# Raw x^T of the first token group by DMA transposes from DRAM, with eight h chunks on it and six on normalized x

## The chip, the cores and the metric

The kernel runs on one core of a Trainium2 chip. The metric is device time in microseconds; the number compared is the median over runs. One further execution was recorded by the profiler, and all views of the profile are of that one.

## The reference

The input x has 2048 tokens of 448 features in bf16. Both branches work on the same layer-normalized x, and the result of one gates the other:

```
xn  = layernorm(x)
q, k, v = split(xn @ wqkv)               # 16 heads of 28
pq, pk  = phi(q), phi(k)                 # phi(t) = (t > 0 ? t + 1 : exp(t)) + 1e-6
s   = (pq @ (pk^T v)) / (pq . sum(pk)) @ wo      # per head, not causal
h   = relu(xn @ w1 + b1)^2               # 1792 wide
g   = silu(h @ w2 + b2)
out = x + s * g
```

## The kernel before

**Tiling.** The 2048 tokens are 16 tiles of 128 (`x_tok[:, si]`), four groups of four. Features lie on partitions in four slices: three of 128 and a rest of 64, which is kept twice, on the lower and the upper 64 partitions, so that the rests of two units run as a pair of half-row matmuls. Normalized x (`xn`) is written by DVE (`ln_norm`, L489), its rest is doubled (L498), and DMA transposes issued by SP (L503, two tiles each) turn it into `xT`, which all matmuls of x read. K units (`kk`, L589) make one token tile of k, Q units (`qq`, L611) one 128-feature slice of q for a group, and h chunks (`hh`, L669) one of the fourteen 128-wide slices of h for a group. ACT applies a ReLU (L638, L641) and DVE or ACT squares (L646, L647). `gg(si)` (L1016) multiplies a token tile of h by w2, and DVE takes the sum out of PSUM (L1034 for group 0, L1041 for the others).

**The first group.** So that TensorE needn't wait for the layer norm, all fourteen h chunks of group 0 are computed from x that isn't normalized (raw x). After some warm-up matmuls (`warm`, L1143) TensorE transposes two x tiles at a time against an identity matrix (`raw_transpose`, L687 to L690); DVE and ACT copy the result out of PSUM into `xr` (L697, L702). Chunks 0 to 3 run in two halves of 256 tokens (L663), one after each transpose. The mean is taken out afterwards: `col_sums(p)` (L723 to L732) sums the columns of w1's part p and adds b1, `stat_rows` and `row_transpose` (L798, L805) make rows of means and deviations, and `aug` (L812) adds their product to the chunk. The factor 1/deviation is left out of h, and its square is applied by `gg` of group 0 through `rvar`:

```
out=gs, in0=ps(b)[:, 0:D], scalar=rvar[:, si : si + 1], in1=b2b[:, :], op0=ALU.mult, op1=ALU.add
```

**Order of work.** Every operation is added to a program in an order written by hand at the end of the kernel. TensorE and SP keep that order. ACT, DVE and POOL are ordered by a planner (`schedule`), which simulates with estimated durations and picks, among what is ready, the operation with the least due time (`late`, derived from the TensorE order), or the one whose `prio` is set. PSUM's eight banks are handed out in the same simulation. A queue waits in its order: an instruction that isn't ready holds up all behind it.

**Queues.** SP issues x tiles 0-1 and 2-3, b1row, w1 part 1, x tiles 4-7, w1 parts 2 and 3, the K and Q weights (wk, wq) and b1r, and after them the transposes as they come due. ACT issues w1 part 0 only. (Part p of w1 holds the columns of chunks 4p to 4p+3.) Token s of partition p is row p*16 + s of x.

Of the kernel before, what the change touches and what calls it, by code (L numbers as in the profile page):

```python
# [9 lines left out]
P = 128  # L10
# [18 lines left out]
class Op:  # L29
    def __init__(self, eng, emit, reads, writes, dur, alts, nbytes):  # L30
        self.eng, self.emit, self.dur, self.alts, self.nbytes = eng, emit, dur, alts, nbytes
        self.reads, self.writes = list(reads), list(writes)
        self.raw, self.deps, self.succ = set(), set(), []
        self.start = self.end = None
        self.seq = None
        self.late = 1e9
        self.prio = None
        self.sync = None
        self.fence = False


class Program:
# [5 lines left out]
    def __init__(self):  # L48
        self.ops, self.writer, self.readers = [], {}, {}
        self.aliases = {}  # L50

# [3 lines left out]
    def add(self, eng, emit, reads=(), writes=(), dur=0.2, alts=(), nbytes=0):  # L55
        reads = [p for r in reads for p in self.aliases.get(r, (r,))]
        op = Op(eng, emit, reads, writes, dur, alts, nbytes)
        for t in op.reads:
            w = self.writer.get(t)
            if w is not None:  # L60
                op.raw.add(w)
            self.readers.setdefault(t, []).append(op)
        for t in op.writes:
            w = self.writer.get(t)
            if w is not None and w is not op:
                op.deps.add(w)
            for r in self.readers.get(t, ()):
                if r is not op:
                    op.deps.add(r)
            self.writer[t] = op  # L70
            self.readers[t] = [r for r in self.readers.get(t, ()) if r is op]
        op.raw.discard(op)
        op.deps |= op.raw
        for d in op.deps:
            d.succ.append(op)
        self.ops.append(op)
        return op

    def schedule(self):
# [6 lines left out]
        for op in reversed(ops):  # L86
# [6 lines left out]
            op.late = late - op.dur - LAT if op.prio is None else op.prio  # L93
# [40 lines left out]
        while n:  # L134
# [69 lines left out]
            if op.nbytes:  # L204
# [72 lines left out]
def bass_recurrent_scan__linear_attn_block__dense_activation_squared_relu__prompt_kernel(  # L277
    nc, A_x, A_wqkv, A_wo, B_x, B_w1, B_b1, B_w2, B_b2, out
):
    with ExitStack() as es:  # L280
# [10 lines left out]
        ones = sb("ones", [P, 1], bf)  # L291
        onesr = sb("onesr", [1, P], bf)
# [8 lines left out]
        xr = sb("xr", [P, 4, 512], bf)  # L301
        xT = sb("xT", [P, NT, 4, P], bf)
# [62 lines left out]
        vset(onesr[:, :], 1.0, "onesr")  # L365
# [6 lines left out]
        vset(bsel[:, 3:5], 1.0, "bsel", True)  # L372
        add(
# [35 lines left out]
        x_r = A_x[0].rearrange("(p s) d -> p s d", s=NT)  # L409
        o_r = out[0].rearrange("(p s) d -> p s d", s=NT)  # L410

        def dma(eng, dst, src, writes, nbytes, reads=(), dur=0.45):
            add(eng, lambda e, _: e.dma_start(dst, src), reads, writes, dur, nbytes=nbytes)

        def load_x(lo, hi, eng="sp"):
            dma(eng, x_tok[:, lo:hi, :], x_r[:, lo:hi, :], [("x", i) for i in range(lo, hi)], (hi - lo) * P * D * 2)
# [29 lines left out]
        load_x(0, 2)  # L446
        load_w1(0, "act", "act")
        load_x(2, 4)
        dma("sp", b1row[:, :], B_b1.rearrange("(o f) -> o f", o=1), ["b1row"], F * 2)
        load_w1(1, "sp", "sp")  # L450
        load_x(4, 8)
        load_w1(2, "sp", "sp")
        load_w1(3, "sp", "sp")
        load_k("sp", w_qkv, A_wqkv, "wk", D, 2 * D)
        load_k("sp", w_qkv, A_wqkv, "wq", 0, D)
        dma("sp", b1r[:, :], B_b1.rearrange("(f p) -> f p", p=P), ["b1r"], F * 2)
# [39 lines left out]
        def x_transpose(lo, hi):  # L496
# [11 lines left out]
            )  # L508
# [41 lines left out]
        def pe_two(a, b, close=True):  # L550
# [10 lines left out]
            if close:  # L561
                a[3]()
                b[3]()

# [70 lines left out]
        def h_out(b, g, fi):  # L635
            slot = r2[:, fi, g * 512 : (g + 1) * 512]
            if g == 0:
# [12 lines left out]

        def hh(g, fi, full=True):
            b = Buf("H")

            def mm(e, rw, c, start, stop, part=None):
# [4 lines left out]
                if g == 0:  # L659
                    rhs = xr[rw, c, :]  # L660
                    if part is not None:
                        t = slice(256 * part, 256 * part + 256)
                        return e.matmul(  # L663
                            ps(b)[:, t], lhs, xr[rw, c, t], start=start and part == 0, stop=False,
                            skip_group_check=True,
                        )
                else:
                    rhs = xT[rw, 4 * g : 4 * g + 4, c, :]
                return e.matmul(ps(b)[:, 0:512], lhs, rhs, start=start, stop=stop)  # L669

            reads = (["xr"] if full else []) if g == 0 else xnames(g)
            return b, reads + w1names(fi // 4), mm, lambda: h_out(b, g, fi), 512

        def raw_transpose(lo):
            bs = [Buf("T"), Buf("T")]
            t = slice(lo * P, lo * P + 256)

            def f(e, _):
                last = None
                for i, b in enumerate(bs):  # L680
                    v = ps(b)[:, :].bitcast(bf)
                    for c in (2 * i, 2 * i + 1):
                        for k in (0, 1):
                            o = ((c - 2 * i) * 2 + k) * P
                            xs = x_tok[:, lo + k, :]
                            if c < 3:
                                last = e.transpose(v[:, o : o + P], xs[:, c * P : (c + 1) * P], ident[:, :])  # L687
                            else:
                                e.transpose(v[:, o : o + P], xs[:, 320:448], ident[:, :])
                                last = e.transpose(v[0:64, o : o + P], xs[:, 384:448], ident[:, :])  # L690
                return last

            add("pe", f, [("x", lo), ("x", lo + 1), "ident"], bs, 0.6)
            vs = [ps_bf(b) for b in bs]
            add(
                "dve",
                lambda e, _: e.tensor_copy(xr[:, 0:2, t], vs[0]()[:, 0:512].rearrange("p (c k) -> p c k", c=2)),  # L697
                [bs[0]], [("xr", lo, 0)], 0.42,
            ).prio = 0
            add(  # L700
                "act",
                lambda e, _: e.activation(  # L702
                    out=xr[:, 2:4, t], in_=vs[1]()[:, 0:512].rearrange("p (c k) -> p c k", c=2), func=AF.Copy
                ),
                [bs[1]], [("xr", lo, 1)], 0.6,
            ).prio = 0
# [4 lines left out]
        def col_sums(p):  # L711
# [30 lines left out]
            )  # L742
# [7 lines left out]
            )  # L750
# [40 lines left out]
        def row_transpose():  # L791
# [13 lines left out]
            add("dve", lambda e, _: e.tensor_copy(rowT, v()[:, 0:512]), [b], ["rowT"], 0.42).prio = 0  # L805
# [18 lines left out]
        def token_sum(c):  # L824
# [26 lines left out]
            add("dve", ev, [b], [("at", c)] + [("xr", lo, i) for lo in (0, 2) for i in (0, 1)], 0.62, alts=[("act", 0.54)])  # L851
# [154 lines left out]
        def gg(si, b=None, part=None):  # L1006
            b = b or Buf("G")
            g = si // 4
            fis = range(NF) if part is None else part

            def f(e, _):
# [3 lines left out]
                for fi in fis:  # L1015
                    last = e.matmul(  # L1016
                        ps(b)[:, 0:D], r2[:, fi, si * P : (si + 1) * P], w_2[:, fi, :],
                        start=(fi == 0 and part is None), stop=(fi == NF - 1),
# [4 lines left out]
            add("pe", f, rd + ([b] if fis[0] else []), [b], len(fis) * MM(D) + (0.19 if part is not None else 0))  # L1023
# [7 lines left out]
            elif g == 0:  # L1031
# [5 lines left out]
                    [b, "b2b", "rvar"], [("g", si % NGB)], 0.65,  # L1037
                )
# [16 lines left out]
        def ss(i, final):  # L1055
# [21 lines left out]
            for b, si in zip(bufs, tiles):  # L1077
# [10 lines left out]
                dma("sp", o_r[:, si, :], ob, [("out", si)], P * D * 2, [("o", si % NOB)])  # L1088

        def ss_last(early, mid):  # L1090
# [13 lines left out]
            def main(k):  # L1104
# [23 lines left out]
                dma("sp", o_r[:, si, lo:hi], o[:, lo:hi], [("out", si, lo)], P * w * 2, [("ol", k)])  # L1128
# [8 lines left out]
        def warm(n, after=()):  # L1137
            b = Buf("W")

            def f(e, _):  # L1140
                last = None
                for _i in range(n):
                    last = e.matmul(ps(b)[:, 0:P], ident[:, :], ident[:, :], start=True, stop=True)  # L1143
                return last

            add("pe", f, ["ident", *after], [b], n * 0.06)
# [12 lines left out]
        def ln(lo, hi, stats=True, step=2):  # L1159
# [4 lines left out]
            for si in range(lo, hi, step):  # L1164
                for k in range(si, si + step):
                    ln_norm(k)
                x_transpose(si, si + step)

        warm(36)
        raw_transpose(0)  # L1170
        col_sums(0)
        H0 = {fi: hh(0, fi, fi >= 4) for fi in range(NF)}
        pr.alias("xr", [("xr", lo, i) for lo in (0, 2) for i in (0, 1)])
        xa = [[("xr", lo, i) for i in (0, 1)] for lo in (0, 2)]
        pe_four(*(H0[i] for i in range(4)), close=False, part=0, need=xa[0])
        raw_transpose(2)
        for si in range(4):
            ln_stats(si)
        ln_rstd(0, 4)
        stat_rows()  # L1180
        col_sums(1)
        pe_four(*(H0[i] for i in range(4)), close=False, part=1, need=xa[1])
        pe_two(H0[4], H0[6], close=False)
        row_transpose()
        aug([H0[i] for i in range(4)], range(4), True)
        for si in (0, 2):
            for k in (si, si + 1):
                ln_norm(k)
            x_transpose(si, si + 2)
        pe_two(H0[5], H0[7], close=False)  # L1190
        aug([H0[i] for i in range(4, 8)], range(4, 8))
        load_x(8, 12)
        ln(4, 8)
        col_sums(2)
# [3 lines left out]
        pe_four(*(H0[i] for i in range(8, 12)), close=False)  # L1198
        aug([H0[i] for i in range(8, 12)], range(8, 12))
# [3 lines left out]
        col_sums(3)  # L1203
        pe_two(H0[12], H0[13], close=False)
        aug([H0[12], H0[13]], (12, 13))
        quads("K0.0 K0.1 Q0.0 Q0.1 K0.2 K0.3")
        for g in (1, 2, 3):
            if g < 3:
                ln(4 * g + 4, 4 * g + 8)
# [90 lines left out]
```

## Time and profile before

| | |
|---|---|
| median of 12 runs | 156.93 us (156.52 to 157.41) |
| the profiled execution | 157.39 us |
| its span, first to last instruction | 155.7 us |
| TensorE matmul busy | 149.2 us, 96% |
| DVE, ACT, POOL busy | 94.4, 76.3, 35.1 us |
| first K and Q units on TensorE | 24.46 us |
| first h chunk of group 1 | 29.72 us |

Busy time is that of one engine. The chain of waits goes back from the last instruction, at each step to what released it; a line of it gives the start, the length, the engine, the tile and the line. A line of a DMA issue gives the time that the queue took to issue it, and from issue to landing.

### The profile page before, as it was taken

To read this page: it belongs to the slowest core of one execution; us is meant where nothing else is said; L and a number is where in the kernel's file an instruction comes from. 1 tells how busy PE (TensorE), PEld (TensorE's weight loads), DVE (VectorE), ACT (ScalarE), POOL (GpSimd) and SP (SyncE) were. 2 spreads that over 40 slices of the span, in tenths; PEclk is the share of its full clock that TensorE was granted. 3 is DMA by queue.
4 is the path that set the end of the run, shared out by engine and by line. 5 is a ranking of instruction groups with operands and counts; after the bars stand their busy time and mean duration, and the time that the engine had idled before them with its cause. 6 is when DMAs were issued, how large, how long until landed. Compare 5 with 4: busy or idle time off the path is not lost.

```text
span 155.7 us, 2915 instructions
## 1 busy us (share of the span) xinstructions
PE 149.2 (96%) x1155; PEld 72.0 (46%) x1155; DVE 94.4 (61%) x237; ACT 76.3 (49%) x146; POOL 35.1 (23%) x54
## 2 busy tenths in 40 slices
PE   5998999999999999999999999989999999999990
PEld 5774445444343444434443454444454445454450
DVE  3377988899897667453689710079764424424473
ACT  3130965699887289380997322989411121111100
POOL 7860000096300027100370000000005505043200
PEclk9999999999999999999999999999999999999998
DMA  4996909993006370000000000000000101020132
GB/s 116 352 298 165 215 15 199 359 275 78 0 0 67 72 135 0 4 0 0 0 6 2 0 0 0 4 0 0 0 4 29 58 30 54 5 63 0 59 102 75
DMA packets 17995, 11.06 MB, mean 71 GB/s; under 512 B 9469, under 2 KB 17597, under 8 KB 17982
## 3 DMA queue, kind: packets, MB, share of 16 engines
q1 hardware_dynamic: 17422, 10.42, 26.3%
q10 hardware_dynamic: 560, 0.46, 0.9%
q8 instruction: 9, 0.15, 0.4%
q14 instruction: 4, 0.03, 0.1%
HBM read 6.95 MB, written 1.84 MB: 56 GB/s over the span
## 4 chain that ended last, share of the span: by engine, by line
PE 94%; ACT 2%; DVE 1%; issue 0%; POOL 0%; DVEq 0%; POOLq 0%
PE pb L1016 28%; PE pb L669 26%; PE pb L589 7%; PE pb L611 6%; PE pb L831 6%; PE pb L1065 5%; PE pb L1143 3%; PE pb L663 2%; PE pb L626 1%; PE pb L1070 1%; PE pb L917 1%; PE pb L837 1%; PE pb L812 1%; PE pb L687 1%; PE pb L723 1%; ACT pk L567 1%
## 5 line engine op out<-in xcount | busy, mean ns | idle before, releaser
L1016 PE MATMUL pb<-w,r 128*128 128x448 bf16 x224 | 44.8, 353 | 0.0
L669 PE MATMUL pb<-xT,w 64*128 64x512 bf16 (+1 forms) x234 | 32.2, 377 | 0.6 <-DVE kvm L871 0.4
L1016 PEld LDWEIGHTS pb<-w,r 128*128 128x128 bf16 x224 | 20.8, 98 | 20.9 <-issue 2.3
L641 ACT ACTIVATE r<-pb,b1f 128x512 bf16<-128x512 f32 x42 | 25.9, 690 | 6.7 <-PE pb L669 6.7
L646 DVE TENSOR_TENSOR r<-r 128x512 bf16<-128x512 bf16 x40 | 16.5, 434 | 14.5 <-ACT r L641 14.0
L1051 ACT ACTIVATE gbuf<-gbuf 128x448 bf16<-128x448 bf16 x15 | 8.6, 581 | 29.6 <-DVE gbuf L1041 29.6
L1084 POOL TENSOR_TENSOR obuf<-obuf,x_tok 128x448 bf16<-128x448 bf16 x10 | 10.1, 1034 | 52.8 <-DVE obuf L1081 52.8
L599 POOL TENSOR_TENSOR zacc<-zacc,pk 128x448 f32<-128x448 f32 x13 | 14.1, 1084 | 34.5 <-DVE pk L579 34.0
L669 PEld LDWEIGHTS pb<-xT,w 64*128 64x128 bf16 (+1 forms) x234 | 11.7, 94 | 16.0 <-issue 0.8
L1041 DVE TENSOR_TENSOR gbuf<-pb,b2b 128x448 bf16<-128x448 f32 x11 | 6.9, 625 | 16.1 <-PE pb L1016 16.1
L589 PE MATMUL pb<-w_qkv,xT 64*128 64x448 bf16 (+1 forms) x106 | 14.3, 350 | 0.0
L567 ACT ACTIVATE pk<-pb 128x448 bf16<-128x448 f32 x16 | 7.9, 542 | 9.0 <-PE pb L589 8.9
L1081 DVE TENSOR_TENSOR obuf<-pb,gbuf 128x448 bf16<-128x448 f32 x14 | 8.3, 621 | 5.3 <-PE pb L1070 5.2
L611 PE MATMUL pb<-xT,w_qkv 64*128 64x512 bf16 (+1 forms) x78 | 11.1, 377 | 0.0
L470 DVE BATCH_NORM_STATS2 st<-x_tok 128x6 f32<-128x448 bf16 x16 | 9.2, 611 | 1.7 <-DMA x_tok<-in_A_x_dram 1.7
L638 ACT ACTIVATE r<-pb 128x512 bf16<-128x512 f32 x14 | 7.3, 597 | 5.7 <-PE pb L812 5.7
L579 DVE SCALAR_TENSOR_TENSOR pk<-pb,pk 128x448 bf16<-128x448 f32 x16 | 9.7, 618 | 0.3
L647 ACT ACTIVATE r<-r 128x512 bf16<-128x512 bf16 x16 | 9.5, 635 | 0.0
L831 PE MATMUL pb<-pk,xn 128*128 128x448 bf16 x48 | 9.4, 353 | 0.0
L572 DVE TENSOR_SCALAR pk<-pk 128x448 bf16<-128x448 bf16 x16 | 6.5, 416 | 4.4 <-ACT pk L567 4.3
L1065 PE MATMUL pb<-msb,pqT 128*128 128x448 bf16 x42 | 9.1, 353 | 0.0
L589 PEld LDWEIGHTS pb<-w_qkv,xT 64*128 64x128 bf16 (+1 forms) x106 | 5.7, 94 | 6.4 <-issue 1.7
(125 smaller groups left out, 160.5 us busy)
## 6 DMA issues: line engine op xcount, KB each, us to landing
out_dram<-obuf SPq DMA_DIRECT2D x15, 112.0 KB, 1.7
w<-in_B_w_dram SPq DMA_DIRECT2D x1, 1568.0 KB, 7.9
x_tok<-in_A_x_dram SPq DMA_DIRECT2D x3, 448.0 KB, 3.6
w_qkv<-in_A_wqkv_dram SPq DMA_DIRECT2D x3, 336.0 KB, 5.1
w<-in_B_w_dram SPq DMA_DIRECT2D x2, 384.0 KB, 5.7
x_tok<-in_A_x_dram SPq DMA_DIRECT2D x2, 224.0 KB, 4.1
w_o<-in_A_wo_dram SPq DMA_DIRECT2D x1, 392.0 KB, 9.5
w<-in_B_w_dram ACTq DMA_DIRECT2D x1, 384.0 KB, 4.4
```

The costliest lines, as they stand in the source:

```text
L579: lambda e, _: e.scalar_tensor_tensor(out=slot, in0=ps(buf)[:, 0:n], scalar=1.0 + 1e-6, in1=slot, op0=ALU.add, op1=ALU.max),
L589: return e.matmul(ps(b)[:, 0:D], xT[rw, si, c, :], w_qkv[rw, c, D : 2 * D], start=start, stop=stop)
L599: lambda e, _: e.tensor_tensor(out=o[:, :], in0=pk[:, 0, :] if i == 1 else zacc[:, :], in1=pk[:, i, :], op=ALU.add),
L611: return e.matmul(ps(b)[:, 0:512], w_qkv[rw, c, m * P : (m + 1) * P], xT[rw, 4 * g : 4 * g + 4, c, :], start=start, stop=stop,)
L641: rl = lambda e, _: e.activation(out=slot, in_=ps(b)[:, 0:512], func=AF.Relu, bias=b1f[:, fi : fi + 1])
L646: return e.tensor_tensor(out=slot, in0=slot, in1=slot, op=ALU.mult)
L647: return e.activation(out=slot, in_=slot, func=AF.Square)
L669: return e.matmul(ps(b)[:, 0:512], lhs, rhs, start=start, stop=stop)
L831: last = e.matmul(ps(b)[:, 0:D], xn[:, si, c * P : (c + 1) * P], pk[:, si, :], start=(si == 0), stop=(si == NT - 1),)
L1016: last = e.matmul(ps(b)[:, 0:D], r2[:, fi, si * P : (si + 1) * P], w_2[:, fi, :], start=(fi == 0 and part is None), stop=(fi == NF - 1),)
L1065: last = e.matmul(ps(b)[:, 0:D], pqT[:, c, si * P : (si + 1) * P], msb[:, c, :], start=(c == 0), stop=False)
L1084: fin = lambda e, _, ob=ob, si=si: e.tensor_tensor(out=ob, in0=ob, in1=x_tok[:, si, :], op=ALU.add)
```

## The change

Raw x^T of group 0 comes by three DMA transposes out of DRAM, issued first on SP: tokens 0 to 255 of all four slices, then features 320 to 447 of all 512 tokens (`xru`, whose upper half is the rest on the upper partitions), then tokens 256 to 511. The source's rows of 512 elements run 64 elements past the end of each token; that part of `xr` isn't read. The TensorE transposes and their copies are gone. The first four token tiles are now rows si*128 + p of x, the rest keep 12 rows per partition, and the output follows. b1row, w1 part 0 and x tiles 0-3 are issued by ACT.

Only chunks 0 to 7 of group 0 use raw x with the correction; chunks 8 to 13 run on `xT` with b1 in the ReLU, as in the other groups, and are woven in between K units. `gg` of group 0 therefore makes two sums in two PSUM banks, chunks 0 to 7, scaled by `rvar`, and chunks 8 to 13, which a second DVE operation adds.

The halves of chunks 0 to 3 run as full-row matmuls (`pe_part`), chunks 5 and 7 are split so that the row transpose and the correction stand between their parts, and the warm-up is 60 matmuls on a tile of zeros. The planner gets a fixed flight time for transposes, subtracts a transfer's flight and a `lead` from due times, and the layer norm of group 0 has a fixed high priority (`hot`). wq and w1 part 3 are issued behind the transposes of group 0.

```diff
+        def raw_t(lo, hi):
+            src = lambda off, n: bass.AP(
+                tensor=A_x.tensor, offset=A_x.offset + off + lo * D, ap=[[D, hi - lo], [1, n]]
+            )
+            add(
+                "sp", lambda e, _: e.dma_start_transpose(xr[:, :, lo:hi], src(0, 512)), [], [("xr", lo // 256)], 1.25,
+                nbytes=(hi - lo) * 1024,
+            )
+        def raw_tu():
+            src = bass.AP(tensor=A_x.tensor, offset=A_x.offset + 320, ap=[[D, 512], [1, P]])
...
-        load_x(0, 2)
+        raw_t(0, 256)
+        dma("act", b1row[:, :], B_b1.rearrange("(o f) -> o f", o=1), ["b1row"], F * 2)
         load_w1(0, "act", "act")
-        load_x(2, 4)
-        dma("sp", b1row[:, :], B_b1.rearrange("(o f) -> o f", o=1), ["b1row"], F * 2)
+        load_x(0, 2, "act")
+        load_x(2, 4, "act")
+        raw_tu()
+        raw_t(256, 512)
         load_w1(1, "sp", "sp")
         load_x(4, 8)
+        dma("sp", b1r[:, :], B_b1.rearrange("(f p) -> f p", p=P), ["b1r"], F * 2)
+        load_k("sp", w_qkv, A_wqkv, "wk", D, 2 * D)
         load_w1(2, "sp", "sp")
...
+        def pe_part(us, part, need):
+            def f(e, _):
+                for u in us:
+                    for k in range(3):
+                        u[2](e, slice(0, 128), k, k == 0, False, part)
+                for i in (0, 1):
+                    us[i][2](e, slice(0, 64), 3, False, False, part)
+                    last = us[2 + i][2](e, slice(64, 128), 3, False, False, part)
...
+        raw = lambda g, fi: g == 0 and fi < 8
...
+                add(
+                    "dve", lambda e, _: e.tensor_tensor(out=gs, in0=ps(bb[1])[:, 0:D], in1=gs, op=ALU.add),
+                    [bb[1], ("g", si % NGB)], [("g", si % NGB)], 0.624,
+                )
...
-        warm(36)
-        raw_transpose(0)
+        warm(60)
         col_sums(0)
-        pe_four(*(H0[i] for i in range(4)), close=False, part=0, need=xa[0])
-        raw_transpose(2)
-        for si in range(4):
-            ln_stats(si)
-        ln_rstd(0, 4)
+        pe_part([H0[i] for i in range(4)], 0, [("xr", 0), "xru"])
+        pr.hot = -100.0
+        for si in (0, 2):
+            ln(si, si + 2)
         stat_rows()
+        pr.hot = None
+        pe_part([H0[i] for i in range(4)], 1, [("xr", 1), "xru"])
         col_sums(1)
-        pe_four(*(H0[i] for i in range(4)), close=False, part=1, need=xa[1])
         pe_two(H0[4], H0[6], close=False)
         row_transpose()
+        pe_main(H0[5])
         aug([H0[i] for i in range(4)], range(4), True)
-        for si in (0, 2):
-            for k in (si, si + 1):
-                ln_norm(k)
-            x_transpose(si, si + 2)
-        pe_two(H0[5], H0[7], close=False)
+        pe_main(H0[7])
+        pe_tails(H0[5], H0[7], close=False)
         aug([H0[i] for i in range(4, 8)], range(4, 8))
+        load_k("sp", w_qkv, A_wqkv, "wq", 0, D)
+        load_w1(3, "sp", "sp")
         load_x(8, 12)
-        ln(4, 8)
-        col_sums(2)
+        ln(4, 8, lead=3)
...
-        pe_four(*(H0[i] for i in range(8, 12)), close=False)
-        aug([H0[i] for i in range(8, 12)], range(8, 12))
...
-        col_sums(3)
-        pe_two(H0[12], H0[13], close=False)
-        aug([H0[12], H0[13]], (12, 13))
-        quads("K0.0 K0.1 Q0.0 Q0.1 K0.2 K0.3")
+        quads("K0.0 H0.8 K0.1 H0.10 K0.2 H0.9 K0.3 H0.11 Q0.0 Q0.1")
+        quads("H0.12 H0.13")
```

## The prediction

> **What bounds the kernel now.** I read the page's busy shares first, then the chain of waits for the opening 26 us, which is where the change lies, then the DMA view and the table by stage. The page says that TensorE is busy almost from end to end:
>
> ```profile
> PE 149.2 (96%) x1155; PEld 72.0 (46%) x1155; DVE 94.4 (61%) x237; ACT 76.3 (49%) x146; POOL 35.1 (23%) x54
> ...
> PE   5998999999999999999999999989999999999990
> ```
>
> So the end moves by what TensorE no longer has to do, less what it newly waits for. The chain (start, length, engine, tile, line) shows the opening:
>
> ```profile
> 1.58 4.02 PE pb L1143 x36
> ...
> 7.06 0.44 PE pb L723 x12
> ...
> 7.77 1.68 PE pb L663 x28
> 9.45 0.44 PE pb L687 x6
> ...
> 10.49 0.61 ACT xr L702
> ...
> 11.15 1.70 PE pb L663 x28
> 12.85 1.72 PE pb L669 x8
> 14.57 0.34 PE pb L798 x4
> 14.94 0.43 DVE scr L805
> 15.42 0.39 PE pb L812 x4
> 15.81 1.72 PE pb L669 x8
> 17.54 0.33 PE pb L812 x4
> 17.86 0.28 PE pb L723 x12
> ...
> 18.48 3.13 PE pb L669 x28
> 21.60 0.33 PE pb L812 x4
> 21.93 0.28 PE pb L723 x6
> ...
> 22.42 1.72 PE pb L669 x8
> 24.14 0.32 PE pb L812 x2
> ```
>
> Warm-up matmuls until 5.60, TensorE transposes (L687 to L690), column sums (L723 to L732), h chunks (L663, L669), corrections (L812). At 10.49 and 14.94 TensorE waits for a copy out of PSUM. K and Q start at 24.46, and group 1 at 29.72.
>
> The new transposes are on no row yet. The nearest are those of normalized x: first their issue on SP (ns, least/median/most), then the DMA view from 22.9 to 26.4 us, which holds two of them, and one half-microsecond inside it.
>
> ```profile
> L503 SPq DMA_TRANSPOSE xT<-xn x8: 1232/1318/1918, 13.5 to 55.6; - x8
> ...
> DMA packets 2129, 0.59 MB, mean 167 GB/s; under 512 B 2112, under 2 KB 2112, under 8 KB 2129
> ...
> 23.50:24.00 0.50, 0.50 (x4) 0.10 (x2) 0.50 (x3) 0.50 (x2) 0.00 (x0) 1.00 1.13 208
> ```
>
> One transpose of 256 KB is 1056 packets of about 256 B, lands 3.2 to 3.3 us after its issue starts, and keeps all 16 DMA engines full for some 1.55 us (two from 23.05 to 26.1): about 170 GB/s of payload, where plain loads in 4.00 to 4.50 ran at 396.
>
> **The change part by part, TensorE first.**
>
> - *Warm-up.* 60 matmuls on a zero tile that needs one DVE memset (first memset at 0.88) instead of 36 on the identity: start 1.2 instead of 1.58. In the trace all 36 run at 4.02/36 = 0.112 us, and ten transposes take 1.46 from 5.60 but 1.04 from 9.45: TensorE is slow until about 7, though the granted-clock column reads 1.00 throughout. At that pace 60 end at 7.9. The Trainium skill, "TensorE: Matmul & The Clock Gate", Part 1, says that the gate opens after about 3.4 us of activity counted in free-running windows, and that a 128-column matmul then takes 56 ns: opening at 5.6 the 60 end at 6.8, at the earliest, 4.6, at 6.2. I take 7.0, between the row's 7.9 and the rule's 6.2, so useful work starts where it did (7.06): worth 0.
> - *Gone:* the first TensorE transpose (replaced by warm-up); the second, 9.45 to 10.49, 1.04; the wait for the copy, 10.49 to 11.15, 0.66, but column sum 1 ran in its shadow and now costs its own 0.50 (as 17.86 to 18.36 does). Net 1.20.
> - *Row correction:* the chunk-5 matmuls now stand between the row transpose and the correction, so the wait 14.91 to 15.42 is filled: 0.51. If the stat rows are late this is lost.
> - *Chunks 8 to 13 on normalized x:* no column sums 2 and 3 (0.50 + 0.49) and no corrections (0.33 + 0.32): 1.64. Their matmuls are the same (3.13 + 1.72).
> - *The halves of chunks 0 to 3:* 28 half-row matmuls of 256 columns, 14 slots in 1.68; now 12 full and 2 pairs, again 14 slots: 0.
>
> Sum on TensorE: 1.20 + 0.51 + 1.64 = 3.35 us less.
>
> **ACT and DVE.** Gone: two copies each (0.60, 0.42), two ACT copies of about 0.28, two DVE operations of 0.34; six ReLUs go from 597 to 690 ns (+0.55 on ACT). Neither is on the chain there, so 0. Added: group 0's g is now two sums in two PSUM banks, so four more DVE additions of 0.625 (row L1041) = 2.5 us, in the stages where DVE has no room: 28 to 40 us is 12.00 busy of 12. They hide beside 2.75 us of second-layer matmuls each, and DVE has lost 1.5 us of earlier work. Against that, mixing K units with h chunks spreads the load that now stalls TensorE at 32.8 (PEld idle 0.69 for ACT r L641). Ends -0.5 to +1.5; I take +0.1, since of all TensorE waits between 26 and 64 us no one exceeds 0.7.
>
> **The queues.** ACT issues b1row, w1 part 0, then x tiles 0-1 and 2-3: 0.32 + 0.46 + 1.17 + 2 x 0.58 from 0.81, so until 3.9; its table load (1.28) follows and is over by 5.2, before its first copy at about 8. x tiles 0-1 were issued at 0.81 and landed by 4.1; now about 6.5. Statistics (0.62 each), rstd and norms then end near 10 and 12. SP issues three raw transposes. Bounds for one issue: 0.4 (a plain load) to 1.9; I take 1.3, the transposes' median. So SP is at 4.7; w1 part 1 (1.57) 6.3, x 4-7 (0.59) 6.9, b1r 7.5, wk (half of the six in 4.22) 9.6, w1 part 2 (1.73) 11.3; then the two transposes of normalized x, 11.3 and 12.6, and only behind these wq, w1 part 3 and x 8-11, until some 18. Those are wanted after 22.5 and stay hidden; w2, wanted for g at about 39, too.
>
> The DMA engines decide more than the issues. They run at rate from about 2.9. Raw x, 640 KB at 170 GB/s, 3.8 us; w1 part 0 (448 KB) and x 0-3 (448) at some 360 GB/s, 2.5. The first raw piece and the upper tail (384 KB), sharing with ACT's loads, are there at 7.2 to 7.7; chunk half 0 wants them at 7.7. The second piece comes at 9.2, wanted at 9.4; w1 part 1 at 10.5, wanted at 11.1. x 4-7, wk, w1 part 2, 1.25 each: 14.2. Then the two transposes: 15.8 and 17.3, plus some receipt. TensorE, by its sum, reaches K0 at 16.3 and h chunk 8, the first to want all four tiles, at 17.0. So a wait of about 0.6, and 0.1 for the earlier ones: +0.7.
>
> A rule speaks against this: the Trainium skill, "DMA: Bandwidth & Descriptors", "Why small descriptors are slow (HBM only)", says that copies within SBUF escape the small-packet penalty, and that a 256 B descriptor from HBM loses 27%; the section on AXI transactions adds that a piece which doesn't start on 256 B costs extra beats, and rows of 896 B start off it every second time. My row is SBUF to SBUF. By the rule raw x takes 4.9 us, everything behind it comes 1.1 later, and the wait is 1.8: a gain of 1.45. I keep the row, because its packets were already at half a plain load's rate, and leave the rule to the range.
>
> **Sum.** -3.35 + 0.7 + 0.1 = -2.55. The profiled execution took 157.39 with a span of 155.7, 1.69 outside the span, and lies 0.46 above the median. So span 153.15, that execution 154.85, median 154.4.
>
> **The rivals.**
>
> - *All transfers in time* (0.15): no wait, and the stall at 32.8 goes as well: -3.35 - 0.5, median 153.1. For it: most margins are within half a microsecond. Against: full DMA engines until 14 us.
> - *Slower: a transpose out of DRAM costs twice one out of SBUF* (0.20). SP stands 3.9 us later, the engines 3.8. The upper tail lands near 10, and the normalized tiles, queued behind raw x, at 21.1 instead of 17.3. TensorE, wanting them at 17.0, waits about 4.2: +0.85 against the gain, or 157.8; at two and a half times 159.7. It decides from about 1.85 times. For it: no row here reads a transpose from DRAM. Against: plain loads from DRAM reach 396 GB/s, so DRAM is not what is slow.
> - *DVE becomes the bound between 20 and 47 us* (0.12). It must do the same work 3.4 us sooner, plus 0.6 per g, and with earlier priorities for norms evictions come later: 2 us back, 156.4, from 155.5 to 157.5. Against: 4 us of DVE idle time between 6.5 and 28.
> - *Nothing removed that counted* (0.03): if the early idle time only moves, 156.9.
>
> **How the numbers follow.** The likeliest, 0.50, is 154.4, its own range 153.3 to 155.7. Measurement can tell about 0.2%, 0.3 us. Faster: 0.50 + 0.15 + half of the DVE case = 0.71. Slower: most of the doubled transposes and a fifth of the DVE case = 0.22; same 0.07. One in ten below and one above gives 152.6 to 158.2.
>
> **What would show it.** Right: CS0 near 7; no L687-like rows; chunk 8 near 17; group 1's first h chunk near 27; raw transposes of 1.3 us each on SP, landed by 5, 7 and 9. Wrong: raw transposes over 2 us or landing after 10 (doubled case); TensorE idle for DVE between 30 and 50; a start of useful work after 8.

## The result, and the profile after

| | before | after |
|---|---|---|
| median | 156.97 us (156.43 to 157.42) | 155.67 us (155.04 to 156.02) |
| ratio, 95% interval | | 0.9912 [0.9897, 0.9927] |
| the profiled execution, its span | 157.39, 155.7 us | 155.04, 153.3 us |
| first K unit on TensorE | 24.46 us | 17.65 us |
| first h chunk of group 1 | 29.72 us | 27.79 us |
| first `gg` of group 0 | 42.20 us | 39.85 us |

The kernel became 0.9% faster: 1.3 us between the medians, 2.4 us between the two profiled executions. That the two differ is part of the story below.

The page of after, busy time and the rows of slices:

```profile
PE 146.1 (95%) x1099; PEld 70.2 (46%) x1099; DVE 96.7 (63%) x235; ACT 77.2 (50%) x147; POOL 35.2 (23%) x54
...
PE   7879999999999999999999999989999999999990
...
PEclk9999999999999999999999999999999999999999
DMA  3999879993007006000000000000001101010123
```

TensorE is still busy almost from end to end, with 3.1 us less busy time. The chain of waits of after (start, length, engine, tile, line) shows the opening that replaced the one of before:

```profile
0.80 1.34 SPq L433
...
2.20 1.24 SPq L440
...
3.49 6.83 DMA xr<-in_A_x_dram
...
10.37 1.81 PE pb L729 x16
12.18 0.28 PE pb L755 x12
...
14.59 0.40 PE pb L830 x4
14.99 0.65 PE pb L732 x3
15.64 0.36 PE pb L844 x4
...
17.65 0.93 PE pb L653 x8
18.58 0.96 PE pb L733 x8
...
27.04 0.76 PE pb L653 x8
27.79 0.86 PE pb L733 x7
```

The path no longer runs through TensorE transposes and their copies, but through the second raw transpose: SP issues it third, at 3.49, and 6.83 us later, at 10.32, it has landed. Only then can the second half of chunks 0 to 3 run (L729). Between the row transpose (14.59, L830) and the correction (15.64, L844) the chunk-5 matmuls (L732) now stand. K0 starts at 17.65 and chunk 8 at 18.58, directly behind it.

The same in the timeline of TensorE, 5 to 11 us (start, length; in brackets the idle time before it and what ended it):

```profile
6.98 0.35 PE L755 MATMUL pb<-w,csf 128*32 128x128 bf16 x12 [0.67 <-DMA w_1r<-in_B_w_dram]
...
7.48 1.48 PE L729 MATMUL pb<-xr,w 128*128 128x256 bf16 x12
...
10.37 0.83 PE L729 MATMUL pb<-xr,w 128*128 128x256 bf16 x6 [1.08 <-DMA xr<-in_A_x_dram]
```

and the landings of the raw transposes of xr and xru, then those of normalized x in the first 16 us:

```profile
L433 SPq DMA_TRANSPOSE xr<-in_A_x_dram x2: 1299/1322/1345, 0.8 to 3.5; - x2
...
DMA to landing us min/median/max: 5.5/6.2/6.8
```

```profile
L440 SPq DMA_TRANSPOSE xru<-in_A_x_dram x1: 1239/1239/1239, 2.2 to 2.2; - x1
```

```profile
L537 SPq DMA_TRANSPOSE xT<-xn x2: 1907/2006/2106, 11.9 to 14.4; - x2
...
DMA to landing us min/median/max: 3.9/4.7/5.5
```

Raw x landed at 6.3, 7.2 and 10.3 us, the normalized tiles at 17.4 and 18.3.

After that the gain only grows once: 1.93 us at group 1's first chunk (29.72 - 27.79), 2.35 at the first `gg` (42.20 - 39.85), and the same at the end. The step between is the stall of before at 32.8, waiting for ACT evacuations, which is gone. The chain of before, then that of after, from about 30 us on:

```profile
32.17 0.59 ACT r L641
...
32.81 1.04 PE pb L669 x8
...
42.20 2.75 PE pb L1016 x14
```

```profile
30.63 0.86 PE pb L733 x8
...
39.85 2.75 PE pb L1049 x14
```

### The profile page after: what moved, and what is told of

It is laid out like the page before. It is cut to its first block, busy times and chain, and to the rows that moved or that the text cites. A ratio compares the mean times of both kernels' runs of the same rounds, so it can differ in the third digit from the quotient of the medians.

```text
span 153.3 us, 2807 instructions
## 1 busy us (share of the span) xinstructions
PE 146.1 (95%) x1099; PEld 70.2 (46%) x1099; DVE 96.7 (63%) x235; ACT 77.2 (50%) x147; POOL 35.2 (23%) x54
## 4 chain that ended last, share of the span: by engine, by line
PE 88%; DMA 4%; ACT 2%; DVE 2%; SPq 2%; issue 0%; DVEq 0%
PE pb L1049 29%; PE pb L733 25%; PE pb L653 7%; PE pb L675 6%; PE pb L863 6%; PE pb L1103 5%; DMA xr<-in_A_x_dram 4%; PE pb L690 1%; PE pb L1108 1%; PE pb L729 1%; PE pb L949 1%; PE pb L869 1%; ACT r L702 1%; SPq L433 1%; SPq L440 1%; PE pb L892 1%
## 5 line engine op out<-in xcount | busy, mean ns | idle before, releaser
L733 PE MATMUL pb<-xT,w 64*128 64x512 bf16 (+1 forms) x264 | 37.0, 377 | 0.4 <-DVE kvm L903 0.4
L705 ACT ACTIVATE r<-pb,b1f 128x512 bf16<-128x512 f32 x48 | 29.8, 691 | 7.0 <-PE pb L733 6.9
L710 DVE TENSOR_TENSOR r<-r 128x512 bf16<-128x512 bf16 x37 | 17.2, 507 | 10.1 <-ACT r L705 10.0
L733 PEld LDWEIGHTS pb<-xT,w 64*128 64x128 bf16 (+1 forms) x264 | 13.6, 94 | 17.4 <-issue 1.0
L653 PE MATMUL pb<-w_qkv,xT 64*128 64x448 bf16 x112 | 13.3, 350 | 0.3 <-ACT r L702 0.3
L711 ACT ACTIVATE r<-r 128x512 bf16<-128x512 bf16 x19 | 11.1, 645 | 0.0
L675 PE MATMUL pb<-xT,w_qkv 64*128 64x512 bf16 (+1 forms) x72 | 10.0, 377 | 0.0
L733 PE MATMUL pb<-xT,w_1r 64*128 64x512 bf16 x48 | 9.2, 378 | 0.0
L653 PEld LDWEIGHTS pb<-w_qkv,xT 64*128 64x128 bf16 x112 | 5.4, 94 | 6.3 <-issue 0.7
L643 DVE SCALAR_TENSOR_TENSOR pqT<-pb,pqT 128x512 bf16<-128x512 f32 x12 | 8.0, 684 | 0.2
```

Source lines behind the costliest of these rows:

```text
L643: lambda e, _: e.scalar_tensor_tensor(out=slot, in0=ps(buf)[:, 0:n], scalar=1.0 + 1e-6, in1=slot, op0=ALU.add, op1=ALU.max),
L653: return e.matmul(ps(b)[:, 0:D], xT[rw, si, c, :], w_qkv[rw, c, D : 2 * D], start=start, stop=stop)
L675: return e.matmul(ps(b)[:, 0:512], w_qkv[rw, c, m * P : (m + 1) * P], xT[rw, 4 * g : 4 * g + 4, c, :], start=start, stop=stop,)
L705: rl = lambda e, _: e.activation(out=slot, in_=ps(b)[:, 0:512], func=AF.Relu, bias=b1f[:, fi : fi + 1])
L710: return e.tensor_tensor(out=slot, in0=slot, in1=slot, op=ALU.mult)
L711: return e.activation(out=slot, in_=slot, func=AF.Square)
```

## The experiments

The theory after seeing the result: what pays is the split of the h chunks (no corrections and column sums for six of them), which needs the planner's new due times; the DRAM transposes are neutral or cost time, since TensorE now waits for transfers where it transposed before. The rival: the DRAM transposes themselves bring the gain, as my sum had it (1.20 us less on TensorE, against 0.7 of new waits). Each kernel's comparisons are with before, run on the same chip.

**Both kernels once more.** No edit.

> The kernel before once more, for a second profile. In the first pair of profiles the spans differ by 2.4 us (155.7 and 153.3) while the medians differ by 1.3. Theory: executions of one kernel differ by up to 1 us in how the opening runs (warm-up pace), and the first profile of before was a slow one, that of after a fast one: this one shows a span of 154.7 to 155.8, and where it is shorter the difference lies before 7.1 us (column sums 0 start earlier than 7.06). Rival: a profiled execution of before always lies 0.4 above its median: 155.6 to 155.8 again, with the same opening.

> The changed kernel once more, for a second profile. Theory: the opening varies, so the span lies between 153.3 and 154.3, and where it is longer the difference lies before chunk 8 of group 0 (18.50 in the first profile): in the end of the warm-up (6.31) or in the landing of the second raw piece (10.32) and of the transposed normalized tiles (17.4, 18.3). From group 1 on the distances between stages are the same as before. Rival: the jitter is spread over the whole kernel, so that chunk 8 is at 18.5 and the end is later.

Before took 157.34 us (span 155.6), after 155.30 (span 153.5). The two lie as the first profiles did, 2.0 us apart, while the medians stay 1.3 apart. A third profile of after is different:

> The changed kernel on the same chip, to compare the others with: 155.4 to 155.9.

Median 155.82, ratio 0.9922 [0.9895, 0.9949]; this profiled execution took 155.78 (span 154.0), close to its own median. There the second raw piece landed at 10.55, and the transposes of group 1 at 27.38, so that group 1 began at 27.51 instead of 27.04. So executions of after spread by as much as the missing gain, and the first profile of it stands at the lower end of its runs (155.04 is the least of 11), those of before, 157.39 and 157.34, at the upper end of theirs (up to 157.42 in 47).

**The DRAM transposes without the split.** All fourteen chunks use raw x; column sums 2 and 3, the corrections and the single sum in `gg` are back.

```diff
-        raw = lambda g, fi: g == 0 and fi < 8
+        raw = lambda g, fi: g == 0
...
         ln(4, 8, lead=3)
+        col_sums(2)
+        pe_four(*(H0[i] for i in range(8, 12)), close=False)
+        aug([H0[i] for i in range(8, 12)], range(8, 12))
```

> The changed kernel with all fourteen h chunks of group 0 on raw x again (column sums 2 and 3, their corrections and one sum per g as in the kernel before); only the DMA transposes, the queues and the new order of the opening stay. Theory (the transposes pay for themselves and no more): TensorE saves 1.20 + 0.51, and waits 1.1 for the second raw piece and up to 0.7 for w1 part 0, so the time is that of before within 0.5 us: 156.5 to 157.2. Rival (the transposes carry the gain and the split of the chunks costs what it brings): 155.4 to 155.9.

Measured 158.68 us, ratio 1.0112 [1.0088, 1.0137]: slower than before, and outside both expected ranges. The timeline of TensorE shows where:

```profile
18.64 0.82 PE L732 MATMUL pb<-xr,w 64*128 64x512 bf16 x6 [0.16 <-ACT r L702]
...
22.73 0.34 PE L755 MATMUL pb<-w,csf 128*32 128x128 bf16 x6 [0.56 <-DMA w_1r<-in_B_w_dram]
```

Chunk 8 starts at 18.64, against 18.48 in before: up to here the DRAM transposes, with the chunk-5 filler beside them, have gained nothing. Then the last part of w1, queued on SP behind the transposes of normalized x and wq, lands at 22.7 us, and column sum 3 waits 0.56 us for it. The first K and Q unit starts at 25.5, a microsecond later than in before. The order of SP's queue fits the split kernel, where these weights are wanted later. So this run shows the transposes and their queue order together, not the transposes alone.

**The split without the DRAM transposes.** Before with TensorE's transposes, chunks 8 to 13 on `xT`, two sums in `gg`, and before's planner.

```diff
+        raw = lambda g, fi: g == 0 and fi < 8
...
-        col_sums(3)
-        pe_two(H0[12], H0[13], close=False)
-        aug([H0[12], H0[13]], (12, 13))
-        quads("K0.0 K0.1 Q0.0 Q0.1 K0.2 K0.3")
+        quads("K0.0 H0.8 K0.1 H0.10 K0.2 H0.9 K0.3 H0.11 Q0.0 Q0.1")
+        quads("H0.12 H0.13")
```

> The kernel before with TensorE transposes, but only chunks 0 to 7 of group 0 on raw x, chunks 8 to 13 on normalized x woven between the K units, and two sums per g of group 0. Theory (the split carries the gain): 1.64 us of TensorE work less, 0.4 from the better mix of K units and h chunks, 0.4 to 0.8 back for waiting on the transposed normalized tiles, which landed at 18.2 in before where chunk 8 would want them at 18.6 or earlier: 155.2 to 155.9. Rival (the split costs what it brings, because of the second sum on DVE): 156.7 to 157.3.

Measured 161.76 us, ratio 1.0327 [1.028, 1.0374]. The waits (engine, line, what it waited for: us, times, longest) and the clock row of its page:

```profile
PE pb L589 <- DMA xT<-xn: 4.0, 1, 4.0
```

```profile
PEclk9999999659999999999999999999999999999998
```

TensorE gets to K0 early, at 17.35, but DVE writes the norms of group 1 (tiles 4 to 7) late, behind evacuations: the first two are copied by 27.5 and transposed by 30.5, the last two are written at 28.9 to 29.5 and transposed near 33. TensorE stands for 4 us from 26.6, and for two slices its granted clock falls to 0.6 and 0.5: the wait is paid twice. The planner has no due time that accounts for the flight of the transposes.

**The same with the planner's part of the change.** Flight time, lead and fixed priorities (for the layer norm of group 0 and the copies beside it), still without DRAM transposes; and, from the other side, after with the due times of before:

```diff
-            op.late = late - op.dur - LAT if op.prio is None else op.prio
+            flight = op.fixed or (op.nbytes and 2.6 + op.nbytes / 330e3)
+            op.late = late - op.dur - flight - LAT - op.lead if op.prio is None else op.prio
```

> The kernel with TensorE transposes and the eight-six split, now also with the changed kernel's planner: due times less flight and lead, the layer norm of group 0 at high priority. Theory (the split saves and the planner makes it usable; the transposes by DMA save nothing): the 4.0 us wait for the tiles 4 to 7 at 26.6 is gone, group 1's first K unit starts at 26.3 to 27.0, against 27.04 in the changed kernel, and the time is 154.3 to 155.6. Rival (the DMA transposes are what saves): 156.5 or more, with the first K unit of group 1 after 28.

> The changed kernel, with flight and lead taken out of the planner's due times again (the fixed flight of transposes in its simulation and the priority of group 0 stay). Theory (the due times carry the change): the norms of tiles 4 to 7 come late, TensorE waits 2 to 5 us for their transposes at the first K unit of group 1, and the time is 157.5 to 161. Rival (the due times were only trimming, and the early wait of the split alone came from the order of its loads): 155.3 to 156.2.

The first took 155.96 us, ratio 0.9932 [0.9907, 0.9956]: the split and the planner alone give what the whole change gives, within the intervals, although here the planner had put the identity late, so that the warm-up starts at 2.08 instead of 1.58. The second, which differs from after in that line only, took 163.64, ratio 1.0399 [1.0362, 1.0435]:

```profile
PE pb L653 <- DMA xT<-xn: 4.1, 1, 4.1
```

It is the same wait as in the split without the planner, with the same dip of the clock. The due times are no side matter: without them the change would have been 4% slower.

**The raw transposes alone on the queues.** After, with all other loads on SP behind the landed raw transposes; its time counts for nothing, its landings do.

> The changed kernel with every other load issued on SP behind the three raw transposes, the first of them only when all three have landed, so that nothing else is on the queues: the price of a transpose out of DRAM. Theory (a transpose from DRAM costs what one within SBUF does, and its lateness is sharing): landings 3.2 to 3.5 us after issue for the two of 256 KB, the last at about 6.8 to 7.2 instead of 10.3, and 170 GB/s. Rival (a DRAM source is slower by itself, as 256 B reads): the last lands after 8, below 130 GB/s. The kernel's own time is of no interest, since all weights come late.

It took 160.34 us. The landings:

```profile
L433 SPq DMA_TRANSPOSE xr<-in_A_x_dram x2: 1297/1322/1348, 0.8 to 3.5; - x2
...
DMA to landing us min/median/max: 3.5/3.6/3.7
```

Alone, a transpose out of DRAM lands 3.5 to 3.7 us after its issue, against 3.2 to 3.3 for one of normalized x in before. It does not cost twice as much. The 5.0 to 6.8 us in after come from what runs beside it. Nor does it hold the engines longer, though the mean over the stretch, 2 to 7.2 us, is below the 130 GB/s that the rival named:

```profile
DMA packets 2656, 0.66 MB, mean 126 GB/s; under 512 B 2656, under 2 KB 2656, under 8 KB 2656
...
q1 hardware_dynamic: 2656, 0.66, 62.1%
```

The packets took 62.1% of the 16 engines' 5.2 us. By an estimate from these lines all of raw x cost 3.2 us of the engines, some 200 GB/s, where I had put 3.8.

**The best version without DRAM transposes.** The split with the planner, plus the filler (chunk 5 between row transpose and correction), a warm-up on zeros that starts at 1.07, and the identity first on POOL. Beside it the same with all chunks raw.

```diff
         row_transpose()
+        pe_main(H0[5])
         aug([H0[i] for i in range(4)], range(4), True)
-        pe_two(H0[5], H0[7], close=False)
+        pe_main(H0[7])
+        pe_tails(H0[5], H0[7], close=False)
...
-ident[:, :], ident[:, :], start=True, stop=True)
+wz[:, :], wz[:, :], start=True, stop=True)
```

> No transposes from DRAM: the last kernel with TensorE transposes, the eight-six split and the planner's due times, with what else the changed kernel has: chunk 5 between the row transpose and the correction (0.5 us), a warm-up on zeros (still 36), and POOL's identity first, which the planner had put 0.5 us late. Theory (the DMA transposes are worth nothing or less): 154.4 to 155.2, below the changed kernel. Rival (they are worth the 1.2 us that they take off TensorE): 155.9 to 156.6, above it.

> The same as the first of this call (TensorE transposes, due times, chunk 5 as filler, warm-up on zeros), but all fourteen chunks on raw x: what is left of the gain without the split. Theory (the split is worth 1.64 us of TensorE work and 0.4 of better mix): 1.6 to 2.4 above the first, 156.2 to 157.2. Rival (the gain comes from filler and warm-up): within 0.7 of the first.

The first took 154.39 us (154.34 to 154.74), ratio 0.9833 [0.9811, 0.9855]: faster than both kernels, by 1.4 us against after on the same chip (155.82). The second took 156.63, ratio 0.9974 [0.9965, 0.9984]. Their difference, 2.24 us, is what the split is worth where the planner knows of the flight. The chain of the best version:

```profile
1.07 4.00 PE pb L1183 x36
5.07 0.64 PE pb L721 x6
...
6.50 0.61 ACT xr L736
...
9.89 0.61 ACT xr L736
...
10.54 1.70 PE pb L697 x28
...
16.99 0.93 PE pb L621 x8
17.92 0.97 PE pb L703 x8
...
27.15 0.86 PE pb L703 x7
```

It pays for its transposes and waits for both copies, and still stands at K0 at 16.99 us, 0.66 before after.

**Half and half.** The best version with tokens 256 to 511 by two DRAM transposes, the second and third issues of SP, and the first half by TensorE. b1row and x tiles 2-3 were behind them, and w1 part 1 went to ACT's queue.

```diff
         load_x(0, 2)
         load_w1(0, "act", "act")
+        raw_second()
         dma("sp", b1row[:, :], B_b1.rearrange("(o f) -> o f", o=1), ["b1row"], F * 2)
...
-        raw_transpose(2)
```

> The first of this call, with the second half of raw x^T only (tokens 256 to 511) by two DMA transposes out of DRAM, issued second on SP, and w1 part 1 issued by ACT; the first half stays on TensorE, where it lies in the time before the weights land. Theory (a DMA transpose pays where its landing is hidden: it is wanted only at 9): 1.0 to 1.2 below the first, 153.3 to 154.2. Rival (it lands late by sharing here as well, or delays the x tiles): not below the first.

Measured 157.78 us, ratio 1.0049 [1.0028, 1.007]: a miss. The chain has `4.18 5.44 DMA obuf<-in_B_b_dram`: b1row landed at 9.62, column sum 0 waited 3.4 us for it, and the clock fell, so that the half of chunks 0 to 3 behind it took 3.21 us, against 1.81 for the same 16 matmuls in after. This profiled execution, 159.04 us, is one of the slower half: in ten of the 20 runs the mean granted clock was 0.978, as here, and in the other ten, 156.78 to 157.69 us, 0.989. I blamed b1row's place in the queue, and moved it ahead of the transposes:

```diff
+        dma("sp", b1row[:, :], B_b1.rearrange("(o f) -> o f", o=1), ["b1row"], F * 2)
         raw_second()
-        dma("sp", b1row[:, :], B_b1.rearrange("(o f) -> o f", o=1), ["b1row"], F * 2)
```

> The hybrid with b1row issued on SP between x tiles 0-1 and the two DRAM transposes, so that it lands by about 4 us as it does where it is an early load. Theory (the hybrid's loss lay in b1row alone): half 0 of h chunks 0 to 3 starts near 7.2 without a wait before it, TensorE's second block of six transposes (1.04 us) and the wait for the copy (0.65 us) are gone, less 0.5 us for column sum 1 that then stands in the open: about 1.0 us less than split_best's 154.39, so 153.2 to 154.2 us, ratio near 0.979. Rival (transposes and loads share the DMA engines, so what is taken off TensorE comes back as late loads): the second raw piece lands after 8.9 us, or x tiles 2-3, w1 part 1 and the normalized transposes land late enough to make TensorE wait over 1 us before h chunk 8; 154.4 to 156.5 us, no better than split_best.

Measured 157.80 us, ratio 1.0019 [0.9996, 1.0042]. My theory fell. b1row is no longer waited for, and TensorE waits as long for another load, the rest of w1's part 0, which ACT's queue issued at 1.9 us:

```profile
1.90 7.50 DMA w_1r<-in_B_w_dram
...
10.28 3.21 PE pb L732 x16
```

The rival held, that what is taken off TensorE comes back as late loads, though at another load than it named, and the time lies above its range too (154.4 to 156.5). The DMA views of three kernels over the same stretch, 5 to 8.5 us (half, after, best version), show what the engines moved:

```profile
DMA packets 1078, 0.50 MB, mean 142 GB/s; under 512 B 714, under 2 KB 1078, under 8 KB 1078
```

```profile
DMA packets 2226, 0.90 MB, mean 256 GB/s; under 512 B 1612, under 2 KB 2226, under 8 KB 2226
```

```profile
DMA packets 965, 1.12 MB, mean 320 GB/s; under 512 B 88, under 2 KB 842, under 8 KB 965
```

In all three the 16 engines are full or nearly so in nearly every slice. With about two thirds of the packets or more below 512 B they move 142 or 256 GB/s, without them 320. An estimate parts the two cases: a packet of a transpose holds some 250 B (256 KB in 1056), and the prediction's rates are 170 GB/s for these and 360 for loads. By them the 0.90 MB of after need 3.8 us, and they took 3.5, so its loads and transposes share as the rates say. The 0.50 MB of the half-and-half version need 2.0 us and took 3.5. There the loads beside the transposes crawl, and why stays open.

## Why the prediction was right, and where its size was off

The direction was right, and the time lies in the range, at the edge of the likeliest case's own (153.3 to 155.7); the gain was forecast at 2.55 us and is 1.3. By the runs the gain is carried by the split with the planner, not by the transposes that the sum credited as well, and the waits came in another place than forecast. Point by point:

- *Warm-up and start: held.* Sixty matmuls ended at 6.31, which is nearer to the rule's 6.2 than to my 7.0. That early end brought nothing: column sum 0 then waited 0.67 us for w_1r. In the two other profiles of after they took 6.0 and 6.2 us instead of 5.25.
- *TensorE's 3.35 us less: held, nearly term by term.* The second transpose and the wait for its copy, less column sum 1, were worth 1.17 (1.70 gone, 0.53 for the sum; put at 1.20), the row correction 0.48 (1.24 against 0.76; put at 0.51), and the sums and corrections of 1.64 are gone. Without the split the best version takes 2.24 us more (I had put the split at 1.64, and later 0.4 for the stall it relieves). The halves of chunks 0 to 3, put at 0, cost 0.24: 1.81 each, against 1.68 and 1.70. Column sum 0, faster by 0.21, hid that. The 3.1 us of busy time is another sum: it holds the warm-up and leaves out the waits that were filled.
- *The wait of 0.7: too small, and in another place.* I had put 0.6 of it before chunk 8, for the normalized tiles, and 0.1 before. For the tiles TensorE waited not at all (landed at 18.3, chunk 8 at 18.58), since it came later itself. The whole was 1.42 (3.35 - 1.93 at group 1's start): 1.08 for the second raw piece, 0.3 for ACT before K0, 0.2 for the stat rows, and smaller differences. The 0.67 for w_1r used up what the warm-up ended early. The second piece came at 10.3 instead of 9.2; x tiles 0-1 at 7.5 instead of 6.5; the normalized tiles at 17.4 and 18.3 instead of 15.8 and 17.3. The term that was off is the order in which the engines take the bytes, not the rates. The DMA view of after from 2 to 10.5 us, when the second piece has just landed:

```profile
DMA packets 4304, 2.10 MB, mean 247 GB/s; under 512 B 2775, under 2 KB 4280, under 8 KB 4304
...
q1 hardware_dynamic: 3200, 1.18, 66.1%
q10 hardware_dynamic: 1104, 0.92, 44.5%
```

  ACT's queue (q10) has moved its 0.92 MB, and SP's (q1) 1.18 MB, of which raw x is only 0.66. So some 0.5 MB of loads that SP issued behind the second piece moved before it had landed. By the rates (0.66 MB at 170 and 1.44 MB at 360 GB/s) they need 7.9 us, about what the stretch has once the engines get going at 2.2 to 2.6. I had let the second piece wait only for raw x and ACT's loads. At 360 GB/s 0.5 MB are 1.4 us, an estimate that covers the 1.1 by which it came late.
- *DVE and the mixing, +0.1: wrong sign.* It was -0.42: the stall at 32.8 is gone, and the extra sums cost nothing that can be seen. The windows from 34 us on have DVE full, as feared, and TensorE full as well:

```profile
34.00:40.00 6.00, 6.00 (x54) 2.44 (x51) 5.95 (x12) 4.79 (x11) 2.24 (x2) 1.00 0.33 88
40.00:47.00 7.00, 7.00 (x48) 2.95 (x46) 6.96 (x19) 5.67 (x12) 0.00 (x0) 1.00 0.04 7
```

  (The columns are busy us of PE, PEld, DVE, ACT and POOL, then clock, DMA share, GB/s.) The rival in which DVE becomes the bound fell. This miss and that of the waits have opposite signs: that the stages' sum comes so close, 2.35 for 2.55, is in part luck.
- *A transpose from DRAM at twice the price: fell.* Alone it lands 3.5 to 3.7 us after its issue. My sign for it, a landing after 10, was met all the same by the other cause. The rule of the Trainium skill, "DMA: Bandwidth & Descriptors", "Why small descriptors are slow (HBM only)", from which I had worked out 4.9 us for raw x and a gain of 1.45, comes near the measured gain, but not by its mechanism: alone raw x cost some 3.2 us of the engines, by the estimate above. No run here separates the packet size from the transposition.
- *The planner: left out of the sum.* I gave the due times no term, and the runs show that some 8 us hang on them (163.64 against 155.67).
- *Which part earns: wrong in part.* I credited the DRAM transposes with 1.20 us less their waits. With the same split, after_five against split_best, the version that keeps TensorE's transposes is 1.4 us faster. The two differ in queue order, in the warm-up and in the token layout too (the changed kernel reads x tiles 0 to 3 one row at a time, before and the best version two), so the 1.4 belongs to the package; the half-and-half versions point the same way.
- *From the profile to the median: the term that was mis-sized.* For the profiled executions I forecast a gain of 2.55 and it was 2.35. I then took the median of after to lie 0.46 below its profiled execution, as that of before does. It lies 0.63 above it. That is 1.1 of the 1.3 us by which the forecast missed. The profile of before stood at the upper end of its runs. Where executions of one kernel differ is partly to be seen in the opening. The 60 warm-up matmuls of after took 5.25, 5.97 and 6.22 us in its three profiles. With TensorE's transposes, the same ten first ones took 1.46 us in before and 1.38 in before_again, but 0.97 in the split without planner, where the first half of chunks 0 to 3 started at 7.24 instead of 7.77. That fits what the Trainium skill says in "TensorE: Matmul & The Clock Gate", Part 1, that the gate's window runs freely and the same kernel opens at different moments. After's opening ends with a DMA landing, so an early gate gives it nothing, while before can use it. That this makes the gain at the medians smaller than in the first profiles is argued and not shown: no profile caught before at its lower end. It can explain half of the 1.0 us spread of before at most, as far as the profiles go. The 0.53 at chunk 0 is the most that one shows, and in the unsplit best version, where the 36 warm-up matmuls took 3.60 us instead of 4.02, column sum 0 then waited 1.2 us for w_1r.

## What to carry to other kernels

Before a gain on the busiest engine is counted, ask what the replacement lands behind: a transfer that takes 3.6 us alone took up to 8.1 here beside two queues of loads. Loads that are issued behind it count as well, since they moved before it had landed. Work that is removed early pays only if the side engines are told to deliver sooner; here the due times decided between 0.9% faster and 4% slower. And look where a profiled execution stands within the runs before carrying its difference over to medians.

## What had not been expected of the hardware

- A DMA transpose of x out of DRAM was issued in 1.24 to 1.35 us in after. It landed in 3.5 to 3.7 us alone, in 5.0 to 6.8 us in after, in 6.1 and 6.4 us in the first half-and-half version and in 8.1 us in the second, where the full engines moved 142 GB/s.
- In waits of 3.4 us and more the granted clock fell to 0.50, and in each trace that has one it stayed there for 6.8 us. In the second half-and-half version, from the view by stage:

```profile
6.00:10.00 4.00, 0.56 (x20) 0.36 (x20) 0.78 (x3) 0.52 (x1) 3.78 (x7) 0.68 1.18 157
10.00:14.00 4.00, 4.00 (x44) 2.21 (x40) 2.37 (x8) 0.28 (x1) 0.28 (x1) 0.50 1.11 325
```

  The 16 half-chunk matmuls there took 3.21 us, those of after 1.81. The Trainium skill, "TensorE: Matmul & The Clock Gate", Part 1, puts the bound at an idle window of some 3.4 us. The runs agree in part: waits of 3.4 to 5.2 us did it in five kernels (both half-and-half versions, the split without planner, after without the due times, the raw transposes alone), and waits of up to 1.3 us (after, the DRAM transposes without the split) left the clock at 1.00. No trace has a wait in between once TensorE runs. But the clock did not stay up for 3.4 us of idle time. The mean of 0.68 over 6 to 10 us says, if the clock is 1.00 or 0.50, that it fell near 7.4, 1.9 us after the last matmul had ended at 5.5; in the five kernels it fell 1.9 to 2.9 us after it. Where page and trace differ the trace decides: if a window of that length is what counts, it had begun while TensorE was still busy. The 0.989 and 0.978 of the first half-and-half version fit steps of this kind, since 3.4 us at half clock take 0.011 off the mean of a 157 us run, and twice that 0.022 (an estimate).
